# Sliding-window attention with a gated feed-forward behind it: other idle matmuls, a moved attention step, Strassen's scheme from tile 3, earlier weight sums, last stores on two queues

## The chip, the cores and the metric

The kernel runs on one core of one Trainium2 chip. The time is device microseconds of one execution. A core has TensorE (PE, with its weight loads shown as PEld), VectorE (DVE), ScalarE (ACT), GpSimd (POOL) and SyncE (SP), each working through its own instructions in order and waiting on semaphores, and 16 DMA engines that carry the transfers which SP, ACT and POOL issue.

## The reference

Causal attention with a window of 64 positions, 8 batches of 8 heads, 576 positions, head size 64. Its output, as 4608 tokens of 512, goes through two layers with SiLU between them.

```python
    scores = scale * np.matmul(q, k.transpose(0, 1, 3, 2))
    rel = pos[:, None] - pos[None, :]
    mask = (rel >= 0) & (rel < window)
    scores = np.where(mask, scores, -1000000000.0)
    attn = exp(scores - max) / sum
    attn_out = np.matmul(attn, v)
...
    x = attn_out.transpose(0, 2, 1, 3).reshape(B * S, H * D)
    h = x @ w_in                       # 512 -> 2048
    g = h * (1.0 / (1.0 + np.exp(-h)))
    out = g @ w_out                    # 2048 -> 512
```

Inputs and output are float32; the products run in bfloat16 with sums in float32.

## The kernel before, in words

**An order written by a planner.** The kernel does not issue its instructions in the order of its text. It hands each step to a planner (`Plan.add`) with a class, the engines that may do it, an assumed duration, and the steps it depends on. `Plan.run` then plays these durations through and fixes, before anything is built, on which engine and in which place each step stands. A class is a queue: its steps keep their order among themselves, and the planner picks between classes by a rank. After that each engine runs its list in order, whatever the real times are.

**Attention.** The 72 blocks of 64 positions are taken in 19 *visits*: four of 3 blocks, then fifteen of 4. Visit 3 is blocks 9 to 11, visit 4 blocks 12 to 15, and so on. A visit consists of scores on PE (L301; the first three visits add a bias product, L293), the exponential on ACT (L308), from visit 3 on a mask product on DVE (L317), values on PE (L334), then on DVE the reciprocal (L340), the norm (L345) and a transposition into the buffer `bridge` (L353), from which the feed-forward reads. Scores and values use the PSUM banks 0 to 3. Scores need q and k turned by DVE (`turn`, L281 and L283), and these and v come by DMAs that POOL issues (L231, L236, L242, L245), as do w_in (L267, 8 DMAs) and w_out (L271, 8 DMAs). q and k of a batch's first third are loaded by SP and ACT.

**Feed-forward.** The 4608 tokens are nine tiles of 512. Tile j's first layer is 16 output pieces `ft` of four products each (L363), and each piece goes through SiLU on ACT (L369) into a slot of `gall`. Tile 0 needs visits 0 to 2, so its first layer is cut into columns 0 to 383 (visits 0 and 1) and 384 to 575 (visit 2), the latter reaching 64 columns into tile 1. First layers use PSUM banks 4 to 7.

The plain second layer (`add_second`, L372) is 64 products of 512 columns in four banks, which ACT or DVE then copy out (L377). For tile 0 it runs over f outside and m inside, for tile 1 over m outside.

From tile 2 on (`FAST`) the second layer is one level of Strassen's scheme (`add_fast_second`): 112 products of 256 columns (L403) in place of 64 of 512. It needs sums of token blocks (`token_sum`, L395, 16 per tile on DVE, into `gsum`) and, once, sums of weight blocks (`weight_sum`, L388, eight on DVE, into slots 16 to 31 of `gall`). Partial results are kept (`keep_part`, L406) and joined (`join`, L413 and L415) before the stores.

**Idle matmuls.** Before the first data is there, and in short waits until the first layer starts, PE multiplies a zero tile (`warm`, L674), 512 columns each, in PSUM bank 2, 3, 6 or 7.

**Stores.** SP issues all output stores (L381). In the last tile the upper two row blocks go out in halves of 256 columns, the lower two whole.

PE's list around the change, in counts of matmuls, as the built program has it, up to the first products of tile 0, and for the second layer of tile 2:

```
idle 36 | bias 4, scores v0 48 | idle 2 | bias 4, scores v1 48 | values v0 48 | idle 5 |
values v1 48 | idle 2 | bias 4, scores v2 48 | idle 6 | values v2 48 | idle 1 | first layer of tile 0 ...

scores v7 | L403 30 | scores v8 | values v7 | L403 34 | values v8 | L403 21 | scores v9 |
L403 15 | scores v10 | L403 12 | first layer of tile 3, with values v9 and v10 in it
```

Of the kernel before, what the change touches and what calls it, by code (L numbers as in the profile page):

```python
# [15 lines left out]
class Plan:  # L16
# [20 lines left out]
    def add_filler(self, n, cls, us, fn, *args, **kw):  # L37
        for _ in range(n):
            op = self.add(cls, us, None, *args, **kw)
            op["until"], op["fn"] = [op], lambda e, op=op: fn(op)  # L40
        self.count -= n
# [7 lines left out]
    def run(self):  # L49
# [9 lines left out]
        while left:  # L59
# [6 lines left out]
            while moved:  # L66
                moved = False
                for e in engines:
# [49 lines left out]
                    left -= c != "warm"  # L118
# [8 lines left out]
def kernel(ctx, tc, q, k, v, w_in, w_out, out):  # L127
    nc = tc.nc
# [13 lines left out]
    RING = list(range(32, 36)) + list(range(16))  # L142
    FAST = range(2, NTT)
# [21 lines left out]
    gall = keep.tile([128, 36, TT], BF16, name="g")  # L165
# [7 lines left out]
    wsum = gall[:, 16:32].rearrange("p (s f) (x d) -> p s (f x) d", s=4, x=2)  # L173
# [11 lines left out]
                  s=1, v=0, moe=99, warm=200, exp=1, mask=1, inverse=0, norm=0.1, cross=0.2, turn=-1.25, cast=-4,  # L185
# [193 lines left out]
    def store(j, m, lo, hi):  # L379
        r0 = j * TT + m * 128  # L380
        nc.sync.dma_start(out=out[r0:r0 + 128, lo:hi], in_=oall[:, m, lo:hi])  # L381

    def weight_sum(i, f):
        lo, hi = w_out_sb[:, f:f + 4], w_out_sb[:, f + 8:f + 12]
        b11, b12, b21, b22 = lo[:, :, 0:256], lo[:, :, 256:512], hi[:, :, 0:256], hi[:, :, 256:512]
        t = [wsum[:, n, f:f + 4] for n in range(4)]
        a, b = [(b12, b11), (b22, t[0]), (b22, b12), (t[1], b21)][i]
        nc.vector.tensor_sub(out=t[i], in0=a, in1=b)  # L388

    def token_sum(i, f, slot):  # L390
        g = gall[:, slot:slot + 4].rearrange("p (f h) t -> p h f t", h=2)
        a11, a12, a21, a22 = g[:, 0, :, 0:256], g[:, 1, :, 0:256], g[:, 0, :, 256:512], g[:, 1, :, 256:512]
        t = [gsum[:, n, f:f + 2] for n in range(4)]
        a, b = [(a21, a22), (t[0], a11), (a11, a21), (a12, t[1])][i]
        (nc.vector.tensor_sub if i else nc.vector.tensor_add)(out=t[i], in0=a, in1=b)  # L395

    def product(bank, lo, m, f, which, slots, first, last):
        g, r = (lambda h, t: gall[:, slots[f + 8 * h], 256 * t + 128 * m:256 * t + 128 * m + 128]), slice(128 * m, 128 * m + 128)
        w = lambda h, d: w_out_sb[:, f + 8 * h, 256 * d:256 * d + 256]
        lhs, rhs = {1: lambda: (g(0, 0), w(0, 0)), 2: lambda: (g(1, 0), w(1, 0)), 3: lambda: (gsum[:, 3, f, r], w(1, 1)),  # L400
                    4: lambda: (g(1, 1), wsum[:, 3, f]), 5: lambda: (gsum[:, 0, f, r], wsum[:, 0, f]),
                    6: lambda: (gsum[:, 1, f, r], wsum[:, 1, f]), 7: lambda: (gsum[:, 2, f, r], wsum[:, 2, f])}[which]()
        nc.tensor.matmul(ps[:, bank["bank"][0], lo:lo + 256], lhsT=lhs, rhs=rhs, start=first, stop=last, skip_group_check=True)  # L403
# [109 lines left out]
    def add_visit(vi):  # L513
        first = vi["n0"] < NB
        z = "0" if first else ""
        ns = 2 * vi["nb"]
        vi["tile"] = (vi["n0"] + vi["nb"] - 1) // TB
        i = vi["i"]
        bs = sorted({n // NB for n in range(vi["n0"], vi["n0"] + vi["nb"])})
        vi["banks"] = 2 if first else 4  # L520
        s = p.add("s" + z, {"PE": 0.05 * ns + (0.85 if first else 0.1)}, None,
                  need_rows(vi) + e_free.get(i - NES, []) + ([c_bias, c_ident] if first else []),
                  gate=None if first else gate_scores(vi), pool="at0" if vi["n0"] < 9 else "at")
        s["fn"] = lambda _: scores(s, vi)
        ex = p.add("exp" + z, {"ACT": 0.19 + 0.00084 * 256 * ns}, lambda _: expo(s, vi), [s], table="exp")
# [24 lines left out]
    def add_weight_sums():  # L550
        for f in (0, 4):
            for i in range(4):
                tsums.append(p.add("tsum", {"DVE": 0.7}, lambda _, i=i, f=f: weight_sum(i, f),
                                   list(wout.values()) + tsums[-1:] + [x for s in range(16, 32) for x in free_gt.get(s, [])]))
# [36 lines left out]
    def add_fast_second(j, gt):  # L591
# [81 lines left out]
    def warm(op):  # L673
        nc.tensor.matmul(ps[:, op["bank"][0]], lhsT=idle, rhs=idle.unsqueeze(1).to_broadcast([128, 4, 128]),  # L674
# [47 lines left out]
    p.add_filler(12, "warm", {"PE": 0.427}, warm, [c_idle], pool="any", lat=0.0)  # L722
    p.add_filler(60, "warm", {"PE": 0.217}, warm, [c_idle], gate=lambda: moe[0][0]["seen"] is None, pool="any", lat=0.0)
# [6 lines left out]
    gts = {0: {ft: (2 * ft, []) for ft in range(NFT)}, 1: {ft: (2 * ft + 1, []) for ft in range(NFT)}}  # L730
    for f in range(0, NFT, 4):
        for ft in range(f, f + 4):
            add_part(0, [ft], gts[0], 0, 384, 1)
        if f == 0:
            continue
        for ft in range(f - 4, f):
            add_part(0, [ft], gts[0], 384, 576, 1)
    for ft in range(NFT - 4, NFT):
        add_part(0, [ft], gts[0], 384, 576, 1)
# [18 lines left out]
    for j in range(1, NTT):  # L758
        if j == 1:
            add_part(1, range(NFT), gts[1], 64, 256, 1)  # L760
            add_part(1, range(NFT), gts[1], 256, 512, 1)
# [20 lines left out]
        if j == 1:  # L782
            add_weight_sums()
# [31 lines left out]
```

## Time and profile before

| what | value |
|---|---|
| median of three executions | 297.51 us (297.27 to 297.89) |
| the profiled execution | 299.93 us |
| its span, first to last instruction | 298.1 us |
| DMA packets | 32.05 MB, mean 108 GB/s |
| code fetched (instruction queue) | 31 packets, 0.51 MB |

The profile page divides the span into 40 equal slices of 7.45 us. The busy time of PE counts matmuls that wait inside the array, so a busy PE isn't PE at its peak; the granted clock (PEclk) tells how fast it ran. "issue" stands where an engine waited for nothing that the profile shows. What bounds a stage is read from PE's rows in order of time and from the gap ahead of each, with its releaser in the bracket. Engines other than PE may wait at no cost.

### The profile page before, as it was taken

What the parts mean: (1) busy time and instruction counts of PE and PEld (TensorE: products, weight loads), DVE (VectorE), ACT (ScalarE), POOL (GpSimd) and SP (SyncE); (2) the same over time, 40 slices, a digit from 0 to 9 for tenths busy, and PEclk for the clock granted to TensorE, in tenths of its full rate; (3) what the DMA queues carried; (4) which work ended last, traced back from release to release, by engine and by line L of the source; (5) the groups of instructions that cost most, each with busy time, mean ns of one, the idle gap of its engine ahead of it and who ended that gap; (6) DMA issues with size and microseconds to landing.
All of it is one profiled execution on the core that took longest, in us unless ns stands there. A gap on an engine that the chain in (4) does not pass through costs nothing.

```text
span 298.1 us, 9147 instructions
## 1 busy us (share of the span) xinstructions
PE 283.8 (95%) x3976; PEld 183.3 (61%) x3984; DVE 172.5 (58%) x327; ACT 164.3 (55%) x255; POOL 118.0 (40%) x181
## 2 busy tenths in 40 slices
PE   8968999899999979999999999999999999999993
PEld 3534764497544558646874686468647854884582
DVE  3881218450598578996984597469446944333412
ACT  2753781498518751868437834773567346416610
POOL 8865796978988779956700000000000000000000
PEclk9997999999999988999999999999999999999999
DMA  9999999999999999999987003000300030012003
GB/s 146 134 169 199 176 156 163 114 219 195 147 202 191 148 140 137 167 209 124 104 119 208 0 4 121 21 2 4 142 0 4 2 144 1 0 37 106 0 20 123
DMA packets 88712, 32.05 MB, mean 108 GB/s; under 512 B 75872, under 2 KB 83552, under 8 KB 88672
## 3 DMA queue, kind: packets, MB, share of 16 engines
q0 software_dynamic: 81600, 18.00, 66.6%
q1 hardware_dynamic: 6752, 13.08, 13.9%
q8 instruction: 31, 0.51, 0.7%
q10 hardware_dynamic: 320, 0.39, 0.5%
q14 instruction: 9, 0.07, 0.1%
HBM read 36.70 MB, written 9.44 MB: 155 GB/s over the span
## 4 chain that ended last, share of the span: by engine, by line
PE 77%; DMA 14%; POOL 5%; issue 1%; ACT 1%; DVE 0%; POOLq 0%; DVEq 0%
PE ps L363 36%; PE ps L403 29%; DMA w_out_sb<-in_moe_w_out_dram 6%; PE ps L372 5%; PE ps L334 3%; PE ps L301 3%; DMA natk<-in_k_dram 3%; DMA w_in_sb<-in_moe_w_in_dram 3%; DMA natq<-in_q_dram 2%; ACT e L308 1%; POOL vo L242 1%; POOL natq L231 1%; POOL natk L231 1%; POOL w_in_sb L267 0%; POOL w_out_sb L271 0%
## 5 line engine op out<-in xcount | busy, mean ns | idle before, releaser
L363 PE MATMUL ps<-bridge,w_in_sb 128*128 128x512 bf16 (+3 forms) x704 | 128.6, 343 | 0.5 <-DVE ot L377 0.4
L369 ACT ACTIVATE g<-ps 128x512 bf16<-128x512 f32 (+3 forms) x176 | 90.4, 519 | 52.5 <-PE ps L363 51.2
L363 PEld LDWEIGHTS <-w_in_sb 128*128 128x128 bf16 x704 | 67.3, 99 | 61.0 <-issue 5.1
L395 DVE TENSOR_TENSOR gsum<-g 128x512 bf16<-128x512 bf16 x56 | 23.6, 421 | 47.7 <-ACT g L369 47.6
L403 PEld LDWEIGHTS <-gsum 128*128 128x128 bf16 x448 | 43.5, 99 | 5.7
L403 PE MATMUL ps<-g,gsum 128*128 128x256 bf16 x336 | 43.5, 276 | 0.0
L308 ACT ACTIVATE e<-ps 128x2048 bf16<-128x2048 f32 (+1 forms) x19 | 34.0, 1787 | 11.5 <-PE ps L301 11.4
L403 PEld LDWEIGHTS <-g 128*128 128x128 bf16 x336 | 32.3, 99 | 5.0
L317 DVE TENSOR_TENSOR e<-e,mask 128x2048 bf16<-128x2048 bf16 (+1 forms) x16 | 19.1, 1194 | 25.1 <-ACT e L308 25.0
L231 POOL DMA_DIRECT2D natk<-in_k_dram x48 | 28.8, 612 | 11.9 <-DMA vo<-in_v_dram 5.1
L231 POOL DMA_DIRECT2D natq<-in_q_dram x48 | 29.2, 630 | 4.0 <-DMA natk<-in_k_dram 1.8
L242 POOL DMA_DIRECT2D vo<-in_v_dram x32 | 28.7, 908 | 5.2 <-PE ps L334 2.8
L406 ACT COPY part<-ps 128x256 f32<-128x256 f32 x28 | 10.4, 372 | 36.9 <-PE ps L403 36.9
L372 PE MATMUL ps<-w_out_sb,g 128*128 128x512 bf16 x120 | 27.7, 379 | 1.0 <-issue 0.8
L403 PE MATMUL ps<-w_out_sb,g 128*128 128x256 bf16 x224 | 27.6, 278 | 0.0
L353 DVE STREAM_TRANSPOSE bridge<-ob 128x1024 bf16<-128x1024 bf16 (+1 forms) x19 | 22.1, 1174 | 0.2
L415 DVE TENSOR_TENSOR ot<-ps,part 128x256 f32<-128x256 f32 (+1 forms) x35 | 16.1, 470 | 10.4 <-PE ps L403 6.0
L345 DVE TENSOR_TENSOR ob<-ps,rc 128x1024 bf16<-128x1024 f32 (+1 forms) x19 | 21.9, 1159 | 0.3
L372 PEld LDWEIGHTS <-g 128*128 128x128 bf16 x128 | 11.9, 98 | 13.6
L674 PE MATMUL ps<-idle 128*128 128x512 bf16 x52 | 13.8, 415 | 3.7 <-issue 2.3
L334 PEld LDWEIGHTS <-e 128*32 128x32 bf16 x1152 | 11.4, 98 | 9.4 <-issue 4.4
L403 PE MATMUL ps<-g 128*128 128x256 bf16 x112 | 15.6, 274 | 0.0
(56 smaller groups left out, 213.5 us busy)
## 6 DMA issues: line engine op xcount, KB each, us to landing
out_dram<-ot SPq DMA_DIRECT2D x34, 256.0 KB, 2.7
vo<-in_v_dram POOLq DMA_DIRECT2D x32, 128.0 KB, 5.9
natq<-in_q_dram POOLq DMA_DIRECT2D x48, 72.0 KB, 4.7
natk<-in_k_dram POOLq DMA_DIRECT2D x48, 72.0 KB, 4.0
ve<-vo SPq DMA_DIRECT2D x12, 264.0 KB, 4.8
w_in_sb<-in_moe_w_in_dram POOLq DMA_DIRECT2D x8, 256.0 KB, 8.7
w_out_sb<-in_moe_w_out_dram POOLq DMA_DIRECT2D x8, 256.0 KB, 7.8
natq<-in_q_dram POOLq DMA_DIRECT2D x10, 96.0 KB, 6.2
```

What stands on the lines that cost most here:

```text
L231: nc.gpsimd.dma_start(out=nats[kk][b % NK][r, h // 4].rearrange("p c x -> p (c x)").rearrange("p (t x) -> p t x", x=2 * D), in_=(q, k)[kk] ...
L242: nc.gpsimd.dma_start(out=vos[b % NV][:, g, :, 0:D], in_=v[b, :, 128 * g:128 * g + 128].rearrange("h p d -> p h d"))
L308: nc.scalar.activation(out=es[vi["i"] % NES][:, :, 0:ns].rearrange("p j s i -> p j (s i)"), in_=ps[:, op["bank"][0]:op["bank"][0] + 4, 0:6 ...
L317: nc.vector.tensor_mul(e, e, m)
L334: nc.tensor.matmul(pv[32 * j:32 * j + 32, sub // k, sub % k], lhsT=e[:, j, s, 32 * u:32 * u + 32], rhs=w[:, 4 * Q + j].rearrange("p (x i) ...
L345: nc.vector.tensor_mul(obs[vi["i"] % NOB][:, 0:4 * vi["nb"]].rearrange("p s (i x) -> p (s i) x", i=2).rearrange("p (b k) x -> p b k x", b= ...
L353: nc.vector.transpose(out=br.rearrange("p n Q u h i -> p (n Q u h) i"), in_=ob.rearrange("p s (h d) -> p (s h) d", h=2))
L363: nc.tensor.matmul(ps[:, bank["bank"][0], 0:hi - lo], lhsT=w_in_sb[:, c, ft * 128:(ft + 1) * 128], rhs=bridge[:, n0 + lo // 64:n0 + hi // ...
L369: nc.scalar.activation(out=g[:, lo:hi], in_=ps[:, bank["bank"][0], 0:hi - lo], func=ACTF.Silu)
L372: nc.tensor.matmul(ps[:, bank["bank"][0]], lhsT=gall[:, slot, m * 128:(m + 1) * 128], rhs=w_out_sb[:, f], start=(f == 0), stop=(f == NFT - 1))
L395: (nc.vector.tensor_sub if i else nc.vector.tensor_add)(out=t[i], in0=a, in1=b)
L403: nc.tensor.matmul(ps[:, bank["bank"][0], lo:lo + 256], lhsT=lhs, rhs=rhs, start=first, stop=last, skip_group_check=True)
```

## The change

Five things change.

1. The idle matmuls at first have 256 columns, in two classes: 26, then more until the scores of visit 0 are issued; after that 512 columns as before. The built program has 68 of them ahead of the first bias product instead of 36.
2. The values of visit 2 may only be issued after 21 products of tile 0's first layer (`moe[20]`). They stood ahead of all of them.
3. Strassen's scheme begins with tile 3. Tile 2's second layer is plain.
4. The weights' sums come right behind tile 0's second layer. For that, tiles 0 and 1 use even and odd slots of `gall`, the sums lie in even slots, later tiles in odd ones, and `gall` has 40 slots.
5. In the last tile all eight stores are halves of 256 columns, and the planner puts each on SP or on ACT. The built program has six of them on ACT's queue, two on SP's.

The quarters of tile 0's first layer are also put into a slightly different order, and tile 1's pieces come in the order f, f + 8.

```diff
-    RING = list(range(32, 36)) + list(range(16))
-    FAST = range(2, NTT)
+    RING = list(range(33, 40, 2)) + list(range(1, 32, 2))
+    FAST = range(3, NTT)
...
-    gall = keep.tile([128, 36, TT], BF16, name="g")
+    gall = keep.tile([128, 40, TT], BF16, name="g")
...
-    wsum = gall[:, 16:32].rearrange("p (s f) (x d) -> p s (f x) d", s=4, x=2)
+    wsum = gall[:, 0:32].rearrange("p (s f o) t -> p s f o t", s=4, o=2)[:, :, :, 0]
...
-        pv = p.add("v" + z, {"PE": 0.05 * ns + 0.1}, None, [ma] + need_v(vi), pool="two" if vi["banks"] == 2 else "at")
+        pv = p.add("v" + z, {"PE": 0.05 * ns + 0.1}, None, [ma] + need_v(vi), pool="two" if vi["banks"] == 2 else "at",
+                   gate=(lambda: moe[20][0]["seen"] is not None) if i == 2 else None)
...
-        for m in range(4):
-            if last and m < 2:
-                p.add("st", {"SP": 0.45}, lambda _, m=m: store(j, m, 0, 256), [c11], dma=0.4)
-                p.add("st", {"SP": 0.45}, lambda _, m=m: store(j, m, 256, 512), [c12[m]], dma=0.4)
-                continue
-            free_ot[m] = [p.add("st", {"SP": 0.45}, lambda _, m=m: store(j, m, 0, d_model),
-                                [c11, c12[m]] if m < 2 else [c21, c22[m - 2]], dma=0.75)]
+        if last:
+            end = [(2, 0, 256, c21), (3, 0, 256, c21), (2, 256, 512, c22[0]), (3, 256, 512, c22[1]), (0, 256, 512, c12[0]), (1, 256, 512, c12[1])]
+            for m, lo, hi, x in [(0, 0, 256, c11), (1, 0, 256, c11)] + end:
+                p.add("st", {"SP": 0.45, "ACT": 0.45}, lambda e, m=m, lo=lo, hi=hi: store(j, m, lo, hi, e), [x], dma=0.4)
+        else:
+            for m in range(4):
+                free_ot[m] = [p.add("st", {"SP": 0.45}, lambda _, m=m: store(j, m, 0, d_model),
+                                    [c11, c12[m]] if m < 2 else [c21, c22[m - 2]], dma=0.75)]
...
-    p.add_filler(12, "warm", {"PE": 0.427}, warm, [c_idle], pool="any", lat=0.0)
-    p.add_filler(60, "warm", {"PE": 0.217}, warm, [c_idle], gate=lambda: moe[0][0]["seen"] is None, pool="any", lat=0.0)
+    p.add_filler(26, "warm", {"PE": 0.214}, warm, 2, [c_idle], pool="any", lat=0.0)
+    p.add_filler(60, "warm", {"PE": 0.109}, warm, 2, [c_idle], gate=lambda: visits[0]["s"]["seen"] is None, pool="any", lat=0.0)
+    p.add_filler(60, "warm2", {"PE": 0.217}, warm, 4, [c_idle], pool="any", lat=0.0,
+                 gate=lambda: visits[0]["s"]["seen"] is not None and moe[0][0]["seen"] is None)
...
-    gts = {0: {ft: (2 * ft, []) for ft in range(NFT)}, 1: {ft: (2 * ft + 1, []) for ft in range(NFT)}}
+    gts = {t: {ft: (4 * (ft % 8) + 2 * (ft // 8) + t, []) for ft in range(NFT)} for t in range(2)}
...
     add_second(0, gts[0], True)
+    add_weight_sums()
...
-        if j == 1:
-            add_weight_sums()
```

PE's list after the change, in counts of matmuls: up to the first layer of tile 0, from there to the first layer of tile 1, and the second layer of tile 2.

```
idle (256) 68 | bias 4, scores v0 48 | idle 3 | bias 4, scores v1 48 | values v0 48 | idle 5 |
values v1 48 | idle 2 | bias 4, scores v2 48 | idle 9 | first layer of tile 0: 21 | values v2 48 | 107 more

scores v3 | L372 19 | values v3 | L372 27 | scores v4 | L372 15 | values v4 | L372 3 | first layer of tile 1
(before: 19, 29, 12, 4)

scores v7 | L372 16 | scores v8 | L372 10 | values v7 | L372 10 | values v8 | L372 11 | scores v9 |
L372 16 | values v9 | L372 1 | first layer of tile 3
```

POOL's list is the same as before.

More of the change, by code (lines that the diff above doesn't have):

```diff
@@ L117, in run @@
                     order.append((op, e))
-                    left -= c != "warm"
+                    left -= not c.startswith("warm")
                     moved = True
@@ L377, in copy_out, with store @@
         copies[e](out=oall[:, m], in_=ps[:, bank["bank"][0]])
[L379 removed]
+    def store(j, m, lo, hi, e="SP"):
         r0 = j * TT + m * 128
[L381 removed]
+        (nc.scalar if e == "ACT" else nc.sync).dma_start(out=out[r0:r0 + 128, lo:hi], in_=oall[:, m, lo:hi])
     def weight_sum(i, f):
[L384 to L386 removed]
+        lo, hi = (w_out_sb[:, g:g + 4].rearrange("p (f x) d -> p f x d", x=2) for g in (f, f + 8))
+        b11, b12, b21, b22 = lo[:, :, :, 0:256], lo[:, :, :, 256:512], hi[:, :, :, 0:256], hi[:, :, :, 256:512]
+        t = [wsum[:, n, f // 2:f // 2 + 2].rearrange("p f (x d) -> p f x d", x=2) for n in range(4)]
         a, b = [(b12, b11), (b22, t[0]), (b22, b12), (t[1], b21)][i]
@@ L759 @@
         if j == 1:
-            add_part(1, range(NFT), gts[1], 64, 256, 1)
-            add_part(1, range(NFT), gts[1], 256, 512, 1)
+            fts = [f + 8 * h for f in range(8) for h in range(2)]
+            add_part(1, fts, gts[1], 64, 256, 1)
+            add_part(1, fts, gts[1], 256, 512, 1)
         else:
```

28 lines of the change are left out of this document (12 added, 16 removed).

## The prediction

> **What bounds the kernel now.** I read the first lines of the page and its clock row first.
>
> ```profile
> span 298.1 us, 9147 instructions
> PE 283.8 (95%) x3976; PEld 183.3 (61%) x3984; DVE 172.5 (58%) x327; ACT 164.3 (55%) x255; POOL 118.0 (40%) x181
> ...
> PEclk9997999999999988999999999999999999999999
> ```
>
> TensorE (PE) is busy for 95% of the span, so time can only come out of its work, its gaps, its slow clock, or what lies behind its last product. The clock dips in slice 4 and in slices 15 and 16. So I listed PE in order of time around the dips (start, duration, instructions; in the bracket the idle time before and what ended it).
>
> ```profile
> 13.79 1.25 PE L674 MATMUL ps<-idle 128*128 128x512 bf16 x5
> ...
> 16.64 0.21 PE L334 MATMUL ps<-ve,e 128*32 128x66 bf16 x4 [1.24 <-issue]
> ...
> 19.09 1.46 PE L674 MATMUL ps<-idle 128*128 128x512 bf16 x6 [0.42 <-DVE ob L345]
> ...
> 23.39 0.38 PE L674 MATMUL ps<-idle 128*128 128x512 bf16 x1 [2.30 <-issue]
> 23.60 17.52 PE L363 MATMUL ps<-bridge,w_in_sb 128*128 128x384 bf16 x128
> ...
> 106.39 0.68 PE L301 MATMUL ps<-qt,kt 32*128 32x64 bf16 x64
> 109.08 0.33 PE L334 MATMUL ps<-ve,e 128*32 128x66 bf16 x16 [2.00 <-ACT e L308]
> ```
>
> Then I took sums over stretches (stretch, length, busy time and count of PE, PEld, DVE, ACT, POOL, granted clock, DMA share, GB/s).
>
> ```profile
> 16.60:21.11 4.51, 4.02 (x128) 2.32 (x128) 3.73 (x5) 3.61 (x4) 3.19 (x5) 1.00 1.15 172
> 21.11:23.30 2.19, 0.00 (x0) 0.00 (x0) 2.08 (x3) 0.39 (x1) 0.70 (x1) 1.00 1.14 164
> ...
> 24.70:28.10 3.40, 3.40 (x13) 1.60 (x11) 0.00 (x0) 1.44 (x4) 2.04 (x3) 0.50 1.24 205
> ```
>
> ```profile
> 106.90:109.05 2.15, 0.17 (x22) 0.16 (x9) 1.69 (x3) 1.88 (x1) 0.90 (x2) 1.00 1.65 157
> ...
> 110.03:113.45 3.42, 3.42 (x19) 2.44 (x17) 2.41 (x6) 0.37 (x1) 3.42 (x5) 0.50 1.08 73
> 102.39:122.85 20.46, 18.19 (x497) 15.12 (x497) 16.80 (x25) 10.07 (x10) 18.32 (x30) 0.92 1.46 142
> ```
>
> Two gaps of over 2 us are each followed by 3.4 us at clock 0.50, in which half, 1.7 us, is lost. The later gap has a releaser: the values of visit 7 wait for the exponential of visit 8, since both use PSUM banks 0 to 3. The earlier one has none ("issue"), and neither has the 1.24 us stop at 16.64, inside equal matmuls that wait for no semaphore. Between those two stops lie exactly 128 matmuls and 128 weight loads, 256 instructions. The DMA view from 20.0 to 23.3 holds one packet of the instruction queue (packets, MB, share):
>
> ```profile
> q8 instruction: 1, 0.02, 1.8%
> ```
>
> 0.02 MB over 256 is about 64 bytes each. I read both stops as PE waiting for the next piece of its code, which queues behind the loads. The first product's data, the bridge of visits 0 and 1, is there at 18.95 + 1.83 = 20.78, 2.8 us before 23.60 (first row; the others are used further down):
>
> ```profile
> 18.95 1.83 DVE L353 STREAM_TRANSPOSE bridge<-ob 128x768 bf16<-128x768 bf16 x2
> ...
> 20.77 0.32 PE L334 MATMUL ps<-ve,e 128*32 128x66 bf16 x16
> ...
> 22.49 0.98 DVE L353 STREAM_TRANSPOSE bridge<-ob 128x768 bf16<-128x768 bf16 x1
> ```
>
> Elsewhere PE runs without gaps; the first-layer and second-layer pieces of the chain of waits give its pace (start, length):
>
> ```profile
> 44.19 8.31 DMA w_out_sb<-in_moe_w_out_dram
> ...
> 83.32 0.68 PE ps L334 x54
> 84.01 0.16 issue
> 84.17 4.48 PE ps L372 x20
> ...
> 102.46 0.62 PE ps L301 x63
> ...
> 254.80 12.23 PE ps L403 x112
> 267.02 13.81 PE ps L363 x64
> ```
>
> So 512 columns take 216 ns, 256 columns 109 ns, a product of the plain second layer about 0.22 us, one visit's scores 0.62, its values 0.68, a switch of form 0.16. The first of these rows says that the last piece of w_out lands at 52.50.
>
> **The change part by part.** The order below is that of the built programs, counted in matmuls.
>
> *The start.* Before, 36 idle matmuls of 512 columns; after, 68 of 256, 6% fewer columns, so the first scores can come at most 0.3 us earlier; but the second scores wait for a transpose fed by a load, so I take 0 (bounds 0 and -0.3). The added instructions move the seams of the code. The first seam fell after 224 matmuls, among the values of visit 1; after, these 224 end at the head of the five idle matmuls ahead of those values. Its piece was asked for, as I take it, when the previous seam was passed, 256 instructions earlier: in the scores of visit 1 then, in those of visit 0 now, whose rows are
>
> ```profile
> 11.10 0.55 PE L301 MATMUL ps<-qt,kt 32*128 32x64 bf16 x48
> ...
> 12.77 0.55 PE L301 MATMUL ps<-qt,kt 32*128 32x64 bf16 x48
> ```
>
> 12.8 to 16.64 was 3.9 us; from 11.3 that gives 15.2. Four or five idle matmuls (1.1), a switch (0.4) and the values (0.5) end at 17.0, where they ended before: no gain, and 1.4 later if the piece still comes at 16.64. The second seam moves from the first product to 12 products behind it, since nine idle matmuls take the place of the six and the values of visit 2 go behind product 21. From stop to stop 16.64 to 23.39 was 6.75 us; from 15.2 the piece is there at 22.0. The nine idle ones still wait for the 19.09 of the row above and end at 19.09 + 9 x 0.216 = 21.0, over the bridge's 20.78. First product 21.1, thirteenth at 23.0: no stop, no dip. The values of visit 2 now end near 25.2, and DVE's three steps behind them (21.09 to 23.47 in the rows above) at 27.6; the half-tile products that need them follow 27 products of 0.16 later, at 29.5. Without that cover PE would wait for the difference. DVE's reciprocal, which waits for these values, holds up the turns of batch 1, whose load ends a long wait anyway:
>
> ```profile
> 34.30 0.53 DVE L283 STREAM_TRANSPOSE qt<-natq 128x192 uint32<-128x192 uint32 x1 [10.83 <-DMA natq<-in_q_dram]
> ```
>
> *Up to the end of tile 0.* The 128 products were 17.52, less 1.7 of the dip 15.8; with the values of visit 2 (0.7) they end at 37.6. Scores of visit 3 (0.6), 19 products (4.2), values (0.7), 27 products (5.9), scores of visit 4 (0.7) lead to 49.7, two more to 50.1. Products 49 to 64 need the last two pieces of w_out, and the last eight cannot begin before 52.50. Then five products (1.1), the values of visit 4 (0.9), three products (0.7): 55.2, where before the row
>
> ```profile
> 57.56 0.81 PE L372 MATMUL ps<-w_out_sb,g 128*128 128x512 bf16 x3 [0.16 <-issue]
> ```
>
> ends at 58.37. Behind it ScalarE (ACT) copies three banks instead of two before its first activation. I take 2.8 of the 3.2 us. Of the bounds, 2.1 is left if the first piece of code comes at 16.64, and 3.5 is had if the load comes a microsecond sooner. A late load, not the code, now sets this stretch. The weights' sums, eight of 0.68, come here on VectorE (DVE), ahead of two turns that the scores of visit 5 need:
>
> ```profile
> L388 DVE TENSOR_TENSOR g<-w_out_sb 128x1024 bf16<-128x1024 bf16 x4 | 2.7, 676 | 0.0
> ```
>
> ```profile
> 63.35 0.74 DVE L281 STREAM_TRANSPOSE kt<-natk 128x576 uint32<-128x576 uint32 x1
> ```
>
> ```profile
> 71.72 0.71 PE L301 MATMUL ps<-qt,kt 32*128 32x64 bf16 x64
> ```
>
> 64.1 - 2.8 + 5.5 = 66.8, scores at 68.9: hidden, 2.1 us in hand. Their strided operands have no row; the same 1024 elements from PSUM take 1.16 us (below), which would make them 3.9 longer and the scores 1.8 late. Nearest are the contiguous sums of the same shape; I take 0, with +1.8 as the far end.
>
> ```profile
> L345 DVE TENSOR_TENSOR ob<-ps,rc 128x1024 bf16<-128x1024 f32 (+1 forms) x19 | 21.9, 1159 | 0.3
> ```
>
> *Tile 2 without Strassen.* 64 products of 512 columns cost 13.8 where 112 of 256 cost 12.2: +1.6. It takes 16 token sums and the eight weights' sums off DVE there. Before, 20.46 us held 12.2 of products, four scores (2.5), two values (1.4) and 0.4 of switches, 16.5: the other 4.0 are the gap, the dip and a short wait. After, 13.8 + three scores (1.9) + three values (2.0) + switches (0.5) = 18.2; that a values replaces a scores balances later (0.06). Cover for each exponential (1.88): 16, 10 and 16 products of 0.22, at least 2.2 us. Gain 2.3; bounds: 0 if one gap comes back without a dip, 2.8 by the leanest switches.
>
> *Last stores.*
>
> ```profile
> 286.02 8.95 SPq L381 DMA_DIRECT2D out_dram<-ot  x6
> ...
> 293.10 0.42 DVE L415 TENSOR_TENSOR ot<-ps,part 128x256 f32<-128x256 f32 x1 [0.45 <-PE ps L403]
> ```
>
> ```profile
> out_dram<-ot SPq DMA_DIRECT2D x34, 256.0 KB, 2.7
> ...
> out_dram<-ot SPq DMA_DIRECT2D x4, 128.0 KB, 1.7
> ```
>
> The last join ends at 293.52; SyncE (SP) issues until 294.97, because three stores are left, two of 256 KB. After, all eight are halves, six on ACT's queue, and only one is left after that join: two issues of 0.48 less, and a landing up to 1.0 shorter. Gain 1.5 (bounds 1.0 and 2.0). On ACT the first store waits for a join ahead of a part copy, which PE needs only a stage of eight products later; it costs nothing. POOL's order is unchanged.
>
> Sum: 2.8 + 2.3 + 1.5 = 6.6 us. The profiled execution took 299.93 (span 298.1) and would take 293.3 (span 291.5); against the median of 297.51 that is **290.9**.
>
> By the Trainium skill (Runtime: NRT & Kernel Launch, Instruction fetch mechanics) code comes in 16 KiB blocks of 256 instructions while the current one runs, and crossing such a boundary is "mostly hidden". The size agrees with the rows; that it is hidden does not, 2.19 us stand empty at such a seam. By that rule the first of the rivals below would hold.
>
> **The rivals.**
> 1. *The first product does not move.* The page names no releaser, so the hold may be something tied to time and not to the seam, a load for instance. Then product 1 stays at 23.6 with the dip, tile 0 ends where it did, and the 2.8 is gone: 293.7. Against it: the stop inside values that wait for nothing, and the 256.
> 2. *One new wait in tile 2.* Ten products cover 1.88 us of exponential by 0.3 only; if ACT's copies come between, one gap of 2.0 with its dip of 1.7 returns: 294.6.
> 3. *Slower: every visit of tile 2 stalls.* Plain products come in bank order m, ACT copies each finished bank between exponentials, scores and values share banks 0 to 3. If ACT runs late for visits 7, 8 and 9 alike, each costs 2.0 + 1.7: 290.9 + 11.1 = 302.0. Two such stalls already give 298.3, so it decides from the second on. For it: it is the wait seen before, thrice. Against it: 16, 10 and 16 products lie between, where before none did.
> 4. *The load comes sooner,* or the copies cost less: 290.0.
>
> **How the numbers follow.** Forecast 0.62 (289.4 to 292.3 with the bounds of its terms), rival 1 0.14, rival 2 0.08, rival 3 0.08, rival 4 0.08. The range 289.0 to 294.7 holds all but rival 3 and some tails. A measurement tells some 0.2%, 0.6 us, from no change: faster 0.90, slower 0.08 (rival 3), the same 0.02 (a case between 2 and 3).
>
> **What would show it.** No PE gap of over 0.5 us between 17 and 24, the first L363 near 21.1, clock 1.00 there; a short wait of L372 near 50.5 and its end near 55; the same stretch for tile 2 of about 18.2 us without a dip; the last landing 1.8 us behind the last join. Wrong it would be by a gap at the seam all the same, by PE waiting for a turn near 69, or by waits for the exponential in tile 2.

## The result, and the profile after

| | before | changed |
|---|---|---|
| median of 20 executions each | 297.95 us (296.36 to 301.03) | 295.32 us (293.23 to 299.52) |
| ratio of the times | | 0.989 [0.9866, 0.9915] |
| the profiled execution | 299.93 us, span 298.1 | 294.13 us, span 292.4 |

The ratio leaves disturbed executions out, the medians take all. The kernel became faster by 2.6 us, median to median. The two profiled executions are 5.8 us apart, where the prediction's sum was 6.6. So there are two questions: which term of the sum was too large, and why the medians show less than half of it.

The profile after has these first lines and this clock row.

```profile
span 292.4 us, 9098 instructions
PE 282.0 (96%) x3957; PEld 181.3 (62%) x3971; DVE 163.9 (56%) x303; ACT 164.8 (56%) x255; POOL 117.8 (40%) x181
...
PEclk9999999999999999999999999999999999999999
```

No slice shows a slow clock. PE in order of time, start of the changed kernel (start, duration, instructions; in the bracket the idle time before and what ended it):

```profile
13.38 0.55 PE L301 MATMUL ps<-qt,kt 32*128 32x64 bf16 x48
...
14.16 0.31 PE L334 MATMUL ps<-ve,e 128*32 128x66 bf16 x16
17.46 1.24 PE L678 MATMUL ps<-idle 128*128 128x512 bf16 x5 [2.99 <-issue]
```

```profile
21.33 2.10 PE L678 MATMUL ps<-idle 128*128 128x512 bf16 x9 [0.42 <-DVE ob L345]
23.27 3.58 PE L363 MATMUL ps<-bridge,w_in_sb 128*128 128x384 bf16 x21
```

One stop without a releaser is left, 2.99 us instead of 1.24, at the head of the five idle matmuls. The first product comes at 23.27 (23.60 before, with a *slow window* behind it, a stretch of 3.4 us in which the granted clock is 0.50). The second stop of 2.30 is gone, the values of visit 2 stand behind 21 products, and nothing waits there.

The end of tile 0, PE again:

```profile
51.70 3.19 PE L372 MATMUL ps<-w_out_sb,g 128*128 128x512 bf16 x14 [0.16 <-issue]
...
55.77 0.59 PE L372 MATMUL ps<-w_out_sb,g 128*128 128x512 bf16 x2 [0.16 <-issue]
```

It ends at 56.36, 2.0 us ahead of the 58.37 of before. PE did not wait for w_out here. The weights' sums on VectorE and the scores that come next:

```profile
59.64 0.65 DVE L388 TENSOR_TENSOR g<-w_out_sb 128x1024 bf16<-128x1024 bf16 x1
...
65.98 0.77 DVE L281 STREAM_TRANSPOSE kt<-natk 128x576 uint32<-128x576 uint32 x1
```

```profile
69.78 0.71 PE L301 MATMUL ps<-qt,kt 32*128 32x64 bf16 x64
```

The strided sums cost what contiguous ones did, 0.65 to 0.69 us, the last turn ends at 66.75, and the scores at 69.78 wait for nothing. Tile 2's second layer as one stretch (stretch, length, busy time and count of PE, PEld, DVE, ACT, POOL, clock, DMA share, GB/s), and then the end of the kernel on DVE, SP and ACT:

```profile
100.45:118.72 18.27, 17.57 (x443) 9.45 (x448) 13.37 (x15) 8.68 (x7) 15.79 (x26) 1.00 1.62 183
```

```profile
289.01 0.42 DVE L416 TENSOR_TENSOR ot<-ps,part 128x256 f32<-128x256 f32 x1 [0.45 <-PE ps L404]
```

```profile
281.93 5.10 SPq L381 DMA_DIRECT2D out_dram<-ot  x2
```

```profile
286.70 3.11 ACTq L381 DMA_DIRECT2D out_dram<-ot  x5
```

Tile 2 takes 18.27 us instead of 20.46, without a gap. From the end of the last join, 289.43, to the span's end at 292.4 it is 2.9 us; before it was 298.1 - 293.52 = 4.6.

### The profile page after: what moved, and what is told of

It is laid out like the page before. It is cut to its first block, busy times and chain, and to the rows that moved or that the text cites. A ratio compares the mean times of both kernels' runs of the same rounds, so it can differ in the third digit from the quotient of the medians.

```text
span 292.4 us, 9098 instructions
## 1 busy us (share of the span) xinstructions
PE 282.0 (96%) x3957; PEld 181.3 (62%) x3971; DVE 163.9 (56%) x303; ACT 164.8 (56%) x255; POOL 117.8 (40%) x181
## 4 chain that ended last, share of the span: by engine, by line
PE 95%; issue 2%; DVE 1%; ACT 1%
PE ps L363 42%; PE ps L404 26%; PE ps L372 14%; PE ps L678 5%; PE ps L334 4%; PE ps L301 4%; DVE ob L345 1%; PE ps L293 0%; ACT ot L377 0%; ACT L369 0%; DVE ot L416 0%; ACT g L369 0%; DVE rc L340 0%; DVE idle L222 0%
## 5 line engine op out<-in xcount | busy, mean ns | idle before, releaser
L363 PE MATMUL ps<-bridge,w_in_sb 128*128 128x512 bf16 (+3 forms) x704 | 127.0, 340 | 0.8 <-DVE ot L377 0.4
L363 PEld LDWEIGHTS <-w_in_sb 128*128 128x128 bf16 x704 | 66.8, 98 | 57.9 <-issue 1.0
L395 DVE TENSOR_TENSOR gsum<-g 128x512 bf16<-128x512 bf16 x48 | 20.1, 419 | 44.7 <-ACT g L369 44.7
L372 PE MATMUL ps<-w_out_sb,g 128*128 128x512 bf16 x178 | 41.1, 379 | 1.7 <-issue 1.6
L308 ACT ACTIVATE e<-ps 128x2048 bf16<-128x2048 f32 (+1 forms) x19 | 34.0, 1787 | 13.6 <-PE ps L301 13.5
L404 PEld LDWEIGHTS <-gsum 128*128 128x128 bf16 x384 | 37.1, 98 | 4.5
L404 PE MATMUL ps<-g,gsum 128*128 128x256 bf16 x288 | 36.4, 273 | 0.0
L407 ACT COPY part<-ps 128x256 f32<-128x256 f32 x23 | 8.6, 372 | 30.2 <-PE ps L404 27.1
L404 PE MATMUL ps<-w_out_sb,g 128*128 128x256 bf16 x192 | 23.0, 273 | 0.0
L416 DVE TENSOR_TENSOR ot<-ps,part 128x256 f32<-128x256 f32 (+1 forms) x30 | 13.8, 469 | 9.1 <-PE ps L404 4.7
L678 PE MATMUL ps<-idle 128*128 128x256 bf16 (+1 forms) x87 | 14.7, 334 | 4.4 <-issue 3.0
L281 DVE STREAM_TRANSPOSE qt<-natq 128x576 uint32<-128x576 uint32 x12 | 9.1, 759 | 14.5 <-PE ps L301 14.5
L377 ACT COPY ot<-ps 128x512 f32<-128x512 f32 x10 | 5.8, 586 | 16.8 <-PE ps L372 12.8
```

The lines of the kernel that those rows point to most:

```text
L308: nc.scalar.activation(out=es[vi["i"] % NES][:, :, 0:ns].rearrange("p j s i -> p j (s i)"), in_=ps[:, op["bank"][0]:op["bank"][0] + 4, 0:6 ...
L363: nc.tensor.matmul(ps[:, bank["bank"][0], 0:hi - lo], lhsT=w_in_sb[:, c, ft * 128:(ft + 1) * 128], rhs=bridge[:, n0 + lo // 64:n0 + hi // ...
L372: nc.tensor.matmul(ps[:, bank["bank"][0]], lhsT=gall[:, slot, m * 128:(m + 1) * 128], rhs=w_out_sb[:, f], start=(f == 0), stop=(f == NFT - 1))
L678: nc.tensor.matmul(ps[:, op["bank"][0], 0:128 * op["parts"]], lhsT=idle, rhs=idle.unsqueeze(1).to_broadcast([128, op["parts"], 128]), star ...
```

## The experiments

Each was timed on one chip together with the kernel before. On the four chips of this table the kernel before has medians of 299.09, 298.94, 298.84 and 299.17, about 1 us over the 297.95 of the result, so across chips it is the ratios that compare. A *seam* is the place between two pieces of PE's code, a *stop* a wait of PE at one. "Stop" is the first one of PE without a releaser behind 13 us, "first product" the start of the first L363, both of the profiled execution, which for "before again" is the slowest of the twelve.

| kernel | median us (lowest to highest, runs) | ratio to before | stop, first product |
|---|---|---|---|
| before again | 298.66 (297.13 to 303.18, 12) | 0.998 [0.9947, 1.0015] | 2.07, 26.54 |
| part 1 undone | 296.43 (293.97 to 299.33, 12) | 0.989 [0.9861, 0.9918] | 1.27, 22.07 |
| part 2 undone | 298.60 (296.11 to 301.71, 12) | 0.998 [0.9943, 1.0008] | 2.93, 25.43 |
| five late idle matmuls | 293.72 (292.11 to 294.26, 6) | 0.980 [0.976, 0.9844] | 1.85, 22.31 |
| changed kernel, again | 295.99 (294.37 to 298.69, 12) | 0.990 [0.9869, 0.9934] | 3.17, 23.64 |
| visit 9 later | 297.29 (295.84 to 298.78, 12) | 0.995 [0.9918, 0.9982] | 3.19, 23.93 |
| part 3 undone | 295.93 (294.73 to 297.64, 12) | 0.992 [0.9885, 0.9945] | 2.80, 23.60 |
| stores on SP alone | 296.60 (294.72 to 299.07, 12) | 0.993 [0.9893, 0.997] | 2.72, 23.30 |
| 60 idle matmuls | 293.24 (292.45 to 295.09, 6) | 0.982 [0.9777, 0.9861] | 1.67, 21.28 |
| 48 idle matmuls | 293.54 (293.12 to 296.14, 6) | 0.984 [0.98, 0.9882] | 1.63, 21.22 |
| five late ones, four ahead of the seam | 293.25 (292.21 to 295.63, 6) | 0.982 [0.978, 0.9864] | none, 20.65 |
| changed kernel, beside the next | 295.60 (294.89 to 296.56, 6) | 0.988 [0.9845, 0.9912] | 2.50, 22.46 |
| 60 idle matmuls, beside it | 293.54 (292.80 to 294.52, 6) | 0.982 [0.978, 0.9853] | 1.15, 21.01 |

### One part undone at a time

The kernel before, unchanged:

> The kernel before, unchanged, to see how its executions spread. Theory A (the profiled execution of before was an unlucky one): the executions differ in their granted clock; most have fewer than the two dips of that profile (mean clock 0.994 or more), and take 296 to 298 us, those with two dips 299 to 300. Theory B (the spread has nothing to do with the dips): clock 0.988 in nearly all, whatever the time.

Eight of the twelve have a clock of 0.992 to 0.994 (one slow window) and take 297.1 to 299.5 us, three have 0.987 or 0.988 and take 299.4 to 303.2. So time goes with the slow windows, as theory A had it, at times about 1 us over those it named; one window and not none is the rule.

Part 1 undone, the first idle matmuls with 512 columns:

```diff
-    p.add_filler(26, "warm", {"PE": 0.214}, warm, 2, [c_idle], pool="any", lat=0.0)
-    p.add_filler(60, "warm", {"PE": 0.109}, warm, 2, ...)
+    p.add_filler(12, "warm", {"PE": 0.427}, warm, 4, [c_idle], pool="any", lat=0.0)
+    p.add_filler(60, "warm", {"PE": 0.217}, warm, 4, ...)
```

> The changed kernel with its first idle matmuls at 512 columns again (part 1 undone; 32 matmuls fewer, so the first seam of the code falls in the values of visit 1 again instead of ahead of five idle matmuls). Theory A (the code behind the first seam lands at 16.6 to 17.5 whatever is asked, and the idle matmuls behind the seam are what makes the values of visit 1 late): first product near 21.5 to 22 instead of 23.3, time 0.5 to 1.2 us under that of the change, so near 294.3. Theory B (the seam's place doesn't matter): the same as the change, 295.3.

Part 2 undone, the values of visit 2 ahead of the first products:

```diff
-                   gate=(lambda: moe[20][0]["seen"] is not None) if i == 2 else None)
+                   gate=None)
```

> The changed kernel with the values of visit 2 ahead of all first products again (part 2 undone). Theory A (a seam right at the first product is what held it up before): the second seam falls in the values of visit 2, ahead of the first product, PE stops there for 1 to 2.5 us, first product near 24.5 to 25, and the clock dips in more executions: 296 to 298. Theory B (part 2 buys nothing): 295.3 as the change.

Part 3 undone, Strassen's scheme from tile 2:

```diff
-    FAST = range(3, NTT)
+    FAST = range(2, NTT)
```

> The changed kernel with Strassen's scheme from tile 2 on, the weights' sums still behind tile 0: part 3 undone. By the prediction's step its tile 2 stretch goes from 18.3 us back to 20.5: the 1.6 us of extra products are saved, a gap of 2.0 us behind the scores of visit 8 comes back, and mostly a slow window of 1.7 us of loss behind it. Theory A: 2.0 to 2.5 us slower than the changed kernel, median 297.5. Rival D (the gap comes back, but the slow window follows it only sometimes, and the plain form has its own stop in some executions): 0 to 1 us slower, median 295.3 to 296.3.

The second queue of part 5 undone:

```diff
-                p.add("st", {"SP": 0.45, "ACT": 0.45}, ...
+                p.add("st", {"SP": 0.45}, ...
```

> The changed kernel with all eight last stores on SP's queue, still in halves: the second queue of part 5 undone. By the prediction's step two issues of 0.48 us come back behind the last join: from the last join to the end of the span 3.4 to 3.9 us instead of 2.97 (it was 4.6 before the change), median 0.4 to 1.0 us slower than the changed kernel. Rival: the halves alone carry the gain, 2.97 us as it is, same median within 0.3 us.

By the table's ratios part 2 carries most of the gain: without it 0.998 is left, against 0.988 to 0.990 of the changed kernel, some 2.4 us. Its 298.60 is over the 296 to 298 of theory A. Part 1 alone carries nothing (0.989 without it, theory B), although the first product came at 22.07 without it, 1.2 us sooner than in the changed kernel and as theory A had it; the same trace loses 3.8 us at a stop in tile 2 (below). PE without part 2:

```profile
23.16 0.32 PE L334 MATMUL ps<-ve,e 128*32 128x66 bf16 x15 [0.17 <-ACT e L308]
24.80 0.19 PE L334 MATMUL ps<-ve,e 128*32 128x66 bf16 x1 [1.32 <-issue]
...
25.43 4.88 PE L363 MATMUL ps<-bridge,w_in_sb 128*128 128x384 bf16 x29
```

The second seam falls into the values of visit 2 and stops PE for 1.32 us ahead of all products. With part 2 that seam lies behind the first products and costs nothing in the profiled execution. The 25.43 is 1.8 to 3.0 us behind the first product in the changed kernel's three traces (23.64, 23.27, 22.46). The stop makes 1.32 of it, the values that now stand ahead about 0.6; the two were not tried apart. Part 3: without it the gap comes back as expected, but in this execution no slow window follows.

```profile
104.81 0.68 PE L301 MATMUL ps<-qt,kt 32*128 32x64 bf16 x64
107.49 0.32 PE L334 MATMUL ps<-ve,e 128*32 128x66 bf16 x16 [2.01 <-ACT e L308]
```

```profile
100.80:119.93 19.13, 16.83 (x498) 14.43 (x497) 16.78 (x26) 10.18 (x10) 17.48 (x28) 1.00 1.60 152
```

The stretch takes 19.13 us, 0.9 more than 18.27, and the medians on that chip are alike (295.93 and 295.99): rival D. In a second execution of the kernel before, the same gap was followed by a slow window, in which eight products of 0.109 took 1.91 us:

```profile
109.85 0.68 PE L301 MATMUL ps<-qt,kt 32*128 32x64 bf16 x64
112.53 0.38 PE L334 MATMUL ps<-ve,e 128*32 128x66 bf16 x16 [2.01 <-ACT e L308]
...
113.91 1.91 PE L403 MATMUL ps<-w_out_sb,g 128*128 128x256 bf16 x8
```

Part 5, DVE's last join and SP's queue with all eight halves on it:

```profile
289.62 0.42 DVE L416 TENSOR_TENSOR ot<-ps,part 128x256 f32<-128x256 f32 x1 [0.45 <-PE ps L404]
```

```profile
282.53 7.87 SPq L381 DMA_DIRECT2D out_dram<-ot  x8
```

The span of that execution ends at 292.9, 2.9 us behind the join at 290.04, as with two queues: the rival held for the tail, the halves carry this gain. Its median is 0.6 us over that of the changed kernel on the same chip (295.99), more than the rival's 0.3. The tail doesn't show why; the ranges and intervals overlap. Part 4 was not undone on its own.

### Where the code comes in late

Five idle matmuls, begun when the first rows have landed, in place of 68:

```diff
-    p.add_filler(26, "warm", {"PE": 0.214}, warm, 2, [c_idle], ...)
-    p.add_filler(60, "warm", {"PE": 0.109}, warm, 2, [c_idle], ...)
+    late = [c_idle, rows_in[(0, 0, 0, 0)]]
+    p.add_filler(8, "warm", {"PE": 0.427}, warm, 4, late, ...)
+    p.add_filler(60, "warm", {"PE": 0.217}, warm, 4, late, ...)
```

> The changed kernel with only the last few idle matmuls at first: they begin when the first rows have landed, so that there are 5 instead of 68 and both seams move back by 126 matmuls' worth of instructions. Theory A (the seams set the first product): the first seam falls into the scores of visit 2, the values of visits 0 and 1 come without a stop, first product near 20.5 to 21 in spite of a slow clock at first; time 293 to 294.5 and fewer dips. Theory B (the slow clock at first and not the code decides): first product no earlier than 23, and 296 or more.

```profile
16.93 0.23 PE L301 MATMUL ps<-qt,kt 32*128 32x64 bf16 x7
19.01 0.49 PE L301 MATMUL ps<-qt,kt 32*128 32x64 bf16 x41 [1.85 <-issue]
...
22.31 4.38 PE L363 MATMUL ps<-bridge,w_in_sb 128*128 128x384 bf16 x21
```

The stop is now in the scores of visit 2, so little is left to do behind it. The first product, 22.31, lies between the two theories; the median, 293.72, is theory A's and below both kernels. With four idle matmuls put ahead of the seam of this kernel:

```diff
-        s["fn"] = lambda _: scores(s, vi)
+        s["fn"] = (lambda _: fill(s, 4) or scores(s, vi)) if i == 2 else lambda _: scores(s, vi)
```

> The kernel of the late idle matmuls (five instead of 68 ahead of the first scores), with four idle matmuls of 512 columns put ahead of visit 2's bias products, where PE then stood for 1.85 us at the seam and lost another 1.4 us in the slow window that followed. Theory A: the stop falls to about 1.0 us, no slow window at 20.5 to 24, first product where it was (21.9 to 22.3, since the next piece of code comes at its own time), tile 0 1.0 to 1.5 us earlier, median about 292.5, ratio 0.975 to 0.979. Rival B (the code is asked for later when PE arrives later): the stop stays 1.85 us, everything 0.9 us later than with the late idle matmuls alone, 294.5.

The stop is gone altogether, and the first product comes at 20.65, earlier than either theory had it. That is partly luck: the packet of the piece started at 15.14 us, in the trace without the four idle matmuls at 16.59. The piece was not later though PE arrived later, which speaks against B, in one pair of executions; A's 1.2 us don't show in the median, 293.25, either.

The changed kernel again, and with visit 9 out of tile 2:

> The changed kernel as it is, beside the others on one chip. Theory A (its parts do what was worked out in an undisturbed execution, and what is missing of the gain is lost where PE waits for the next piece of its code, at the start each time and in tile 2 in some executions): two groups of executions again, most between 293.2 and 296.5 us at a mean clock of 0.993 to 1.00, and three to five of twelve near 298 us at 0.988; median 295.3. Rival B (the second group is a state of one chip): one group only, near 294.5 us.

```diff
-                  gate=None if first else gate_scores(vi), ...
+                  gate=None if first else (lambda: [x for x in moe if x[3] == 3][15][0]["seen"] is not None) if i == 9 else gate_scores(vi), ...
```

> The changed kernel with the scores of visit 9 held until 16 products of tile 3's first layer are issued, its values 17 products later; in tile 2's second layer two scores and two values are left, so that the 256 instructions ahead of a seam of the code take longer there (about 6 us or more instead of 4.8). Theory A: no stop of PE without a releaser between 100 and 125 us, executions at clock 0.988 become rare (at most one of twelve), the median falls by 0.5 to 1.5 us against the changed kernel on the same chip, to about 294.3. Rival B (the 298 us executions have nothing to do with tile 2): the same groups as the changed kernel, median within 0.4 us of it. Rival C (visit 9 is late for tile 4 or its exponential stalls tile 3): slower by 1 us or more, with a wait for ACT behind 125 us.

The first has most executions under 296.5 us and one of twelve at 298.69, fewer than A's three to five, and its median of 295.99 is over both 295.3 and 294.5. The second has no stop between 100 and 125 us and no execution with two slow windows, but it is slower: rival C, with the wait named there. Waits of PE behind 100 us (us in total, times, longest):

```profile
PE ps L363 <- ACT g L369: 1.6, 1, 1.6
PE ps L334 <- issue: 0.5, 1, 0.5
```

Visit 9's exponential now stands among the SiLUs of tile 3's first layer, and PE runs out of free banks.

The changed kernel itself stops in tile 2 in this second trace (296.20 us), at a seam 12 times 256 instructions behind the first one, amid the values of visit 9. No slow window follows:

```profile
118.74 0.28 PE L334 MATMUL ps<-ve,e 128*32 128x66 bf16 x11
120.57 0.24 PE L334 MATMUL ps<-ve,e 128*32 128x66 bf16 x5 [1.55 <-issue]
```

With part 1 undone it stops one seam sooner, and a slow window follows:

```profile
112.71 0.52 PE L301 MATMUL ps<-qt,kt 32*128 32x64 bf16 x44
115.37 0.39 PE L301 MATMUL ps<-qt,kt 32*128 32x64 bf16 x20 [2.15 <-issue]
115.70 5.20 PE L372 MATMUL ps<-w_out_sb,g 128*128 128x512 bf16 x16
```

A stop of 2.15 us amid scores, then 16 products in 5.20 us in place of the 3.6 at full clock: 3.8 us in all, about the distance between the changed kernel's executions with no slow window and with two (below).

Then the seams alone were moved, by leaving out 8 or 20 of the first idle matmuls and nothing else:

```diff
-    p.add_filler(60, "warm", {"PE": 0.109}, warm, 2, [c_idle], ...
+    p.add_filler(34, "warm", {"PE": 0.109}, warm, 2, [c_idle], ...
```

> The changed kernel with the first eight idle matmuls left out (60 in place of 68) and nothing else: every later instruction comes 16 places earlier, so each seam of the code (every 256 instructions) falls 16 places later in the work. By the times of the changed kernel's trace the shortest stretch of 256 instructions in tile 2 goes from 4.8 to 5.6 us; at the start the five idle matmuls of 512 columns come ahead of the stop instead of behind it (first product 1.2 us earlier, 22.0). Theory A (stops at seams, followed by slow windows, are what is missing): median 1.0 to 2.0 us under the changed kernel, ratio 0.983 to 0.987, executions at clock 0.988 at most one in twelve. Rival B (seams in tile 2 decide nothing; only the start moves): same distribution as the next kernel.

> The same with 20 of the first idle matmuls left out (48): seams 40 places later in the work. The start is like that of 60 idle ones (the stop falls in the values of visit 1 in both), but in tile 2 a stretch of 256 instructions now takes only 3.3 us by the changed kernel's trace (both visits' values close together), less than the 3.3 to 5.5 us which the next piece took there from the crossing to the end of its packet plus 1.4 us. Theory A: a stop of PE without a releaser of 1 to 2.5 us between 105 and 115 us, in many executions with a slow window of 1.7 us behind it; median 1.5 to 3 us over that of 60 idle ones, ratio 0.990 to 0.995. Rival B: within 0.6 us of 60 idle ones, no such stop.

Eight fewer gave 293.24 and no execution with a slow window; 20 fewer 293.54, two of six with one. So B had the medians right. The short stretch of 3.3 us did not stop PE. The kind of stop that A named is there all the same, but one seam later, in the scores of visit 9, and in both kernels, 1.20 and 1.75 us. With 48 a slow window follows it:

```profile
111.97 0.41 PE L301 MATMUL ps<-qt,kt 32*128 32x64 bf16 x31
114.13 0.43 PE L301 MATMUL ps<-qt,kt 32*128 32x64 bf16 x33 [1.75 <-issue]
114.49 5.31 PE L372 MATMUL ps<-w_out_sb,g 128*128 128x512 bf16 x16
```

What eight idle matmuls are worth was then measured side by side:

> The changed kernel as it is (68 idle matmuls at first), on one chip with the next. Theory A: a stop of 2.7 to 3.2 us without a releaser ahead of the five idle matmuls (16.4 to 17.5), first product 23.2 to 24; ratio to before 0.989 to 0.991, some executions at clock 0.988. Rival B (the gain of 60 idle ones was that of another chip): like the next one within 0.5 us.

> The changed kernel with 60 idle matmuls at first, nothing else, on the same chip. Theory A: the stop falls to 1.6 to 2.0 us and lies behind the five idle matmuls, in the values of visit 1; first product 21.2 to 22; mostly no slow window; median 1.5 to 2.5 us under that of 68 idle ones, ratio 0.981 to 0.985. Rival B: median within 0.5 us of it.

```profile
13.85 1.25 PE L678 MATMUL ps<-idle 128*128 128x512 bf16 x5
15.03 0.21 PE L334 MATMUL ps<-vo,e 128*32 128x66 bf16 x3
16.39 0.30 PE L334 MATMUL ps<-vo,e 128*32 128x66 bf16 x13 [1.15 <-issue]
...
21.01 3.58 PE L363 MATMUL ps<-bridge,w_in_sb 128*128 128x384 bf16 x21
...
50.42 2.97 PE L372 MATMUL ps<-w_out_sb,g 128*128 128x512 bf16 x13 [0.61 <-DMA w_out_sb<-in_moe_w_out_dram]
```

295.60 against 293.54 us: 2.1 us for eight matmuls of zeros, theory A, though both stops (2.50 and 1.15) are shorter than it named. The five idle matmuls (1.2 us) now run ahead of the stop instead of behind it, so the same late piece costs less. In the two traces that is 1.5 us, first product and end of tile 0 alike (22.46 and 21.01, 56.33 and 54.82); the rest of the 2.1 is not placed. The 21.01 and the wait for w_out near 50.4 are what the prediction named for the change itself.

## Why the prediction was wrong in size

**The start (2.8 predicted, 2.0 in the profiled pair).** That the stops are seams of the code, 256 instructions apart, held: the stop stood at the head of the five idle matmuls, as the count said (by the lists 223 matmuls lie ahead of it, where the prediction has 224), and leaving out eight moved it by 16 instructions, three values past the idle ones. In 14 of the 15 traces the first stop stands behind 223 matmuls, whatever these are; one has no stop. The values of visit 2 moved behind 21 products at no cost. The step that failed is "from 11.3 that gives 15.2", that a seam passed sooner brings the next piece sooner: PE passed it at 11.67 instead of 12.77, and the piece came later. Its packet lies between 14.9 and 16.2 us of the trace, and PE went on at 17.46. When a piece is asked for, no trace shows. Transfers of the changed kernel, 11.7 to 14.9 us and then 14.9 to 16.2 (queue: packets, MB, share of 16 engines' time):

```profile
q0 software_dynamic: 2482, 0.41, 189.2%
```

```profile
q0 software_dynamic: 741, 0.22, 173.2%
q8 instruction: 1, 0.02, 5.4%
```

The first product then was at 17.46 + 5.81 = 23.27, not 21.1. The end of tile 0 is 1.2 later than forecast (56.36 against 55.2), not 2.2, because PE no longer had to wait for w_out. Of the 2.0 us that were gained only 0.33 is the product's; the other 1.7 lie between it and the end of tile 0, about what the slow window at 24.70 had cost. That none followed the longer stop was luck (last section): in the changed kernel's second trace the stop of 3.17 us was followed by one. The prediction's own bound, "1.4 later if the piece still comes at 16.64", was the right mechanism, 0.8 short. The first rival, that the product does not move, described the first product better than the forecast, though not by its reason, and not the slow window that it kept: the hold is at the seam, and where the seam falls decides what it costs (21.01 to 21.28 with 60 idle ones). By the Trainium skill (Runtime: NRT & Kernel Launch, Instruction fetch mechanics) the crossing of a block is mostly hidden. The profiled execution agrees for all but one of the changed kernel's seams, and disagrees at that one, 2.99 us, where the loads kept the DMA engines full; the second trace disagrees at two, 3.17 and 1.55 us.

**Tile 2 (2.3 predicted).** 18.2 was predicted for the stretch, 18.27 measured; the banks held, no exponential was waited for. The step that failed is what stood on the other side: 20.46 contained a slow window of 1.7, which is not always there. Without it Strassen's scheme takes 19.13 in the one trace that shows it, the gain is 0.9, and the medians can't tell it from none. In some executions the plain form stops at a seam of its own (1.55 us in the second trace).

**The last stores (1.5 predicted)** gave 4.6 - 2.9 = 1.7, all of it from the halves. The step that ACT's queue saves two issues on the path was wrong, SP alone ends as early; that the sum came out near is luck.

**The weights' sums (0 predicted)** cost nothing, 0.65 to 0.69 us each.

**The median.** The largest step that failed is "against the median of 297.51 that is 290.9". The 6.6 held two slow windows of 1.7, and the profiled execution was one of those with two. The mean granted clock of an execution tells how many slow windows it had (about 1.00 none, 0.994 one, 0.988 two; in the table 0.997 and over, 0.990 to 0.996, less). All executions that were recorded with a clock, except for those of altered kernels:

| slow windows | before: executions, median us | changed: executions, median us |
|---|---|---|
| none | 8, 297.85 | 18, 294.73 |
| one | 62, 298.52 | 13, 296.20 |
| two or more | 28, 300.28 | 7, 298.30 |

Like with like the gain is 2.0 to 3.1 us. The chips are mixed there; on the chip with the most executions of both it is 2.4 without a window and 2.2 with one. Before, two windows cost 300.28 - 297.85 = 2.4 us, not the 3.4 of the prediction; why less is open, in the profiled execution PE was busy through both. And two were not what most executions had. The miss of 295.32 - 290.9 = 4.4 us is made of 0.8 by which the profiled pair fell short of the sum (the start; the other two terms cancel), 299.93 - 297.51 = 2.4 from taking the sum of one execution off the median of others, and 295.32 - 294.13 = 1.2 by which the changed kernel's median lies over its profiled execution: it too has slow windows in half of its executions. No trace of the changed kernel near 298 us was taken; that a stop in tile 2 with its slow window accounts for these is argued from the trace with part 1 undone.

**Two workings of the prediction do not come out of its own figures.** The bounds of its terms give 290.9 + 0.7 + 2.3 + 0.5 = 294.4 and 290.9 - 0.7 - 0.5 - 0.5 = 289.2, not 292.3 and 289.4; the measured 295.32 lies outside both. And 0.02 MB over 256 is 78 bytes; the 64 come out of the 0.51 MB of all 31 pieces.

## What to carry to other kernels

Where PE stops without a releaser, count the instructions from stop to stop, and let work that must come first, idle work too, fall ahead of the seam: eight matmuls of zeros fewer were worth 2.1 us of 296. Before a gain is worked out from one trace, look up how often its slow windows occur in the other executions, and take the gain off an execution of the same kind.

## What the runs showed of the hardware

**A slow window came behind half a window of idle time.** The clock changes of a trace lie on a grid of 3.413 us (before: slow windows at 24.70 and at 110.03, 85.33 us or 25 grid steps apart). I took PE's idle time in each grid window of all 15 traces, leaving out the wait for the first rows. All 12 windows with 1.75 us or more of it (half is 1.71) were followed by a window at clock 0.50; none of the 18 others with 0.96 to 1.70 us was. Grid windows as stretches (columns as above), of the changed kernel, of its second execution, and of the kernel with 48 idle matmuls:

```profile
12.62:16.03 3.41, 1.85 (x101) 1.31 (x100) 1.60 (x6) 2.40 (x2) 1.79 (x4) 1.00 1.99 142
16.03:19.44 3.41, 1.98 (x55) 1.02 (x55) 1.01 (x4) 1.26 (x2) 3.41 (x6) 1.00 1.34 164
19.44:22.85 3.41, 2.99 (x62) 1.58 (x61) 3.41 (x5) 1.84 (x2) 2.06 (x4) 1.00 1.17 169
```

```profile
14.05:17.46 3.41, 0.77 (x4) 0.38 (x4) 1.95 (x4) 0.81 (x2) 2.73 (x4) 1.00 1.57 166
17.46:20.87 3.41, 3.41 (x57) 1.42 (x54) 1.76 (x3) 0.89 (x2) 2.79 (x5) 0.50 1.16 164
```

```profile
111.25:114.66 3.41, 1.66 (x69) 0.89 (x68) 1.25 (x1) 0.03 (x1) 2.77 (x4) 1.00 1.96 196
114.66:118.07 3.41, 3.41 (x9) 1.22 (x8) 2.60 (x3) 1.85 (x1) 2.07 (x5) 0.50 1.99 193
```

A stop of 2.99 us was cut by a grid edge into 1.56 and 1.43 and cost no slow window; one of 3.17 lay in one window for 2.64 and cost one. That the grid runs free of the kernel is stated by the Trainium skill (TensorE: Matmul & The Clock Gate, What's actually happening), and the traces agree: counted from the first instruction, its first edge lies anywhere from 0.04 to 3.40 us. So where the grid falls has a part in which executions of one program lose this time, and no idle time of 1.70 us or less within one window cost one here.

**A piece of code was late where the loads were dense.** In tile 2, eleven of the traces have PE at its instruction 3011, a seam, between 106.1 and 108.5 us. The packet of the next piece started between 110.1 and 112.6, with little order between the two (107.8 and 110.49 in one, 107.7 and 112.64 in another). In the changed kernel's stretch from 150 to 290 us, with the loads done and the stores at 13.6% of the DMA engines' time, 13 pieces were fetched:

```profile
q0 software_dynamic: 528, 0.07, 0.7%
q8 instruction: 13, 0.21, 0.6%
```

PE stopped for none of them, and not only because 256 instructions take longer there: from 196.6 to 199.9 us, at a DMA share of 0.00, it got through 293 in 3.3 us without a gap. That it is the loads which hold the code up goes by this contrast; it was not tried by taking loads away.
